# Another table of turns for a fused attention and MLP block on one core

## The chip, the core and the metric

The kernel runs on one core of a Trainium2 chip. Its metric is the device time in microseconds (us) of one execution; lower is better. The engines are named as in the profile: PE is TensorE's matmul (PEld its weight loads), DVE VectorE, ACT ScalarE, POOL GpSimd, SP SyncE, which issues most DMAs.

## The reference

The block normalizes x (2048 tokens, D = 448), computes an attention in four segments of 512 tokens with a memory carried from segment to segment, and a gated MLP beside it, and multiplies the two:

```python
def phi(t): return jnp.where(t > 0, t + 1.0, jnp.exp(t))
for s in range(4):                       # 16 heads of 28
    logits = jnp.einsum('bhqd,bhkd->bhqk', qs, ks) * scale + mask   # causal in the segment
    a_dot = jnp.einsum('bhqk,bhkd->bhqd', _softmax(logits), vs)
    num = jnp.einsum('bhld,bhde->bhle', phi(qs), M)
    den = jnp.einsum('bhld,bhd->bhl', phi(qs), z)[..., None] + 1e-06
    outs.append(g * (num / den) + (1.0 - g) * a_dot)                # g = sigmoid(beta)
    M = M + jnp.einsum('bhld,bhle->bhde', phi(ks), vs); z = z + phi(ks).sum(over l)
s = concat(outs) @ wo
g = silu((gelu(xn @ w_gate) * (xn @ w_up)) @ w_down)                # w_gate: 448 x 1792
return x + s * g
```

## The kernel before

Everything stays in SBUF. A segment has four blocks of 128 tokens; heads are padded from 28 to 32, four to a group of 128 partitions, so there are four groups; the hidden dimension has 14 blocks of 128. PSUM is two pairs of banks (pp) and four single banks (ps). All work is first recorded as 1172 named operations with their dependencies; nothing is emitted then. The function arrange (L158) goes through the table TURNS (L89), one name for each operation, and places every operation at its turn. A suffix such as ":ACT" chooses an engine where two could do it. At its turn an operation also takes its PSUM banks and buffers: of those that its kind may use, the one that by a small cost model comes free first. Then the program emits the operations in that order. The table thereby fixes the order of each engine's own instructions, SP's DMA issues included; every engine works through its instructions in order, and waits at one whose inputs or buffers aren't ready, with all that is behind it on that engine. Engines run freely against each other.

The names that matter here (a number such as 013 is segment 0, hidden block 13; sc07 is segment 0, step 7):

- x1, x2, x3 (L427 for x2 and x3, L353 for x1): the loads of a segment's input, issued by SP. wg8 and wu8 (L353): halves of the gate and up weights. tk and tq (L630), tr (L552): DMA transposes of kT, qT and of the normalized input, also on SP. wo_in (L422), wd_in (L430): the output and down weights.
- bn, ag, ep (L495, L497, L508): statistics, their aggregate and the variance of the layer norm on DVE, pw (L513) the power on POOL, xn (L520) the normalized rows. In segment 0 xc (L530) centres the rows on DVE, and PE transposes these (trc).
- wq, wk, wv (L581): projections in 3 matmuls of 128 rows; wr (L581): the remaining 64 rows. evwq, evwk, evwv (L617): their evacuations. phwq, phwk, miwk (L704 to L709, L696): the two halves of phi.
- sc (L848): scores of one step, four 32-row tiles by two banks; ex (L863): their exponential on ACT; mk (L874): the causal mask on POOL; pv (L910): the product with the values. ou (L746) evacuates the sums.
- gi, gu (L971 in segment 0, L1001 later): gate and up products; ge (L1009): gelu on ACT; hm (L1014): the product of gate and up on DVE, which frees the bank of up. gates: sigmoid of beta on ACT, ahead of the first exponential. dn (L1057, L1123 for the last block): the down product.
- up (L725) updates the memory, rd (L761) reads it; den, dc, rd and rb (L749 to L794) carry the denominators over DRAM; ca, cb (L816, L811 and L819) combine; wo (L1087, L1111) is the output projection, fm, th, sg, fa, y (L1062 to L1142) the tail of a block.
- wo0 (L391): a memset of the output weights' tile; bd0 to bd3 (L417): four small memsets of the mask of the memory. nrm and nrm2: the guard, a check of the weights' norms whose answer the program loads ahead of the last piece of the output (L1184).

## Time and profile before

| what | us |
|---|---|
| median of 3 runs | 225.86 (225.45 to 225.96) |
| the profiled execution | 225.30 |
| its span in the profile | 223.5 |
| DVE busy | 150.9 |
| ACT busy | 158.3 |
| POOL busy | 126.3 |

The profile is one execution. Times in it count from the start of its span; the execution is 1.8 us longer than the span. A row of its timeline has the start, the duration, the engine, the line of the kernel, the operation with output and inputs, the form, how many instructions are joined in the row, and in brackets the idle time of the engine before it and what ended that. Rows of an engine's queue (SPq) are the issues of DMAs, not the transfers.

### The profile page before, as it was taken

Reading aid. Unit: us, or ns where it says so; the run is one execution under the profiler, and the core shown is the slowest. Engines: PE = TensorE matmul, PEld = TensorE weight load, DVE = VectorE, ACT = ScalarE, POOL = GpSimd, SP = SyncE. Lnnn points to the kernel's source line nnn. Section 1 sums busy time; section 2 is a strip of 40 time slices with the busy share of each in tenths; the row PEclk is TensorE's granted clock in tenths of the full one; section 3 lists DMA queues with packets and bytes.
Section 4 is the critical chain, followed back from the end, with each engine's and each line's share of the span. In section 5 each row is a group of like instructions: output and inputs, shape, how many; then the busy total and the mean of one; then the engine's idle time right before and its main releaser. Section 6 shows DMA issues by size and latency. Waiting matters only on the chain.

```text
span 223.5 us, 5109 instructions
## 1 busy us (share of the span) xinstructions
PE 215.4 (96%) x1906; PEld 96.2 (43%) x1906; DVE 150.9 (68%) x285; ACT 158.3 (71%) x218; POOL 126.3 (57%) x219
## 2 busy tenths in 40 slices
PE   7999999899999999999999999999999999999991
PEld 2454343343433354444444444444444434444570
DVE  4586897997779977554688476675835563466472
ACT  5888455899988977959688988744688877436120
POOL 5423100167978889524769995728059767464700
PEclk9999999999999999999999999999999999999999
DMA  6999589896692664326550422083502001448011
GB/s 201 241 345 284 99 126 290 223 164 129 143 130 42 173 177 89 67 67 179 165 133 10 87 64 64 24 221 105 167 21 72 28 14 23 143 120 215 17 45 50
DMA packets 45463, 27.71 MB, mean 124 GB/s; under 512 B 30664, under 2 KB 40840, under 8 KB 45432
## 3 DMA queue, kind: packets, MB, share of 16 engines
q1 hardware_dynamic: 44216, 26.33, 50.9%
q10 hardware_dynamic: 1216, 0.98, 1.3%
q8 instruction: 17, 0.28, 0.5%
q14 instruction: 14, 0.11, 0.2%
HBM read 17.38 MB, written 2.98 MB: 91 GB/s over the span
## 4 chain that ended last, share of the span: by engine, by line
PE 83%; DVE 7%; ACT 4%; issue 2%; DMA 1%; POOL 1%; DVEq 0%; ACTq 0%; POOLq 0%
PE ps L1057 15%; PE ps L1001 14%; PE pp L1001 14%; PE ps L581 12%; PE ps L1087 5%; PE pp L971 5%; PE pp L848 5%; PE ps L971 4%; PE ps L910 4%; ACT pt L863 3%; PE pp L1057 1%; PE ps L761 1%; PE ps L725 1%; DVE st L495 1%; DMA x_sb<-in_A_x_dram 1%
## 5 line engine op out<-in xcount | busy, mean ns | idle before, releaser
L863 ACT ACTIVATE pt<-pp 128x1024 bf16<-128x1024 f32 x76 | 74.0, 1032 | 13.1 <-PE pp L848 12.0
L874 POOL TENSOR_SCALAR_AFFINE_SELECT pt<-pt 128x256 bf16<-128x256 bf16 x128 | 52.7, 443 | 24.0 <-ACT pt L863 23.4
L1057 PE MATMUL ps<-wd_sb,hT 128*128 128x448 bf16 x196 | 41.1, 353 | 0.1
L1014 DVE TENSOR_TENSOR hT<-gl,ps 128x512 bf16<-128x512 bf16 x28 | 18.8, 683 | 19.5 <-ACT gl L1009 19.5
L1009 ACT ACTIVATE gl<-pp 128x512 bf16<-128x512 f32 x28 | 16.6, 597 | 19.6 <-PE pp L1001 14.8
L1001 PEld LDWEIGHTS <-wu_sb 64*128 64x128 bf16 x252 | 23.1, 94 | 14.9
L1001 PEld LDWEIGHTS <-wg_sb 64*128 64x128 bf16 x252 | 23.1, 94 | 14.8 <-issue 1.5
L1057 PEld LDWEIGHTS <-hT 128*128 128x128 bf16 x210 | 19.2, 98 | 20.0 <-issue 3.9
L1009 ACT ACTIVATE gl<-ps 128x512 bf16<-128x512 f32 x28 | 16.5, 596 | 14.0 <-PE ps L1001 9.9
L1014 DVE TENSOR_TENSOR hT<-gl,pp 128x512 bf16<-128x512 bf16 x28 | 18.7, 677 | 7.3 <-ACT gl L1009 7.3
L581 PEld LDWEIGHTS <-xnT 128*128 128x128 bf16 (+1 forms) x192 | 14.4, 96 | 20.3 <-issue 11.4
L772 POOL TENSOR_TENSOR om<-om,rb 128x512 f32<-128x512 f32 x12 | 15.0, 1265 | 13.4 <-DMA rb<-rdr 9.2
L696 POOL TENSOR_SCALAR e<-e 128x896 bf16<-128x896 bf16 (+1 forms) x12 | 11.8, 985 | 15.9 <-ACT e L691 15.9
L819 POOL TENSOR_TENSOR oT<-oa,om 128x512 bf16<-128x512 f32 x12 | 17.3, 1448 | 5.1 <-DVE oa L816 5.1
L513 POOL TENSOR_TENSOR rs<-rs,nhalf 128x1 f32<-128x1 f32 (+1 forms) x7 | 5.3, 763 | 24.7 <-DVE rs L508 24.6
L1001 PE MATMUL ps<-xnT,wg_sb 64*128 64x512 bf16 x66 | 17.8, 377 | 0.0
L1001 PE MATMUL ps<-xnT,wu_sb 64*128 64x512 bf16 x66 | 17.8, 377 | 0.0
L1001 PE MATMUL ps<-xn,wu_sb 64*128 64x512 bf16 x66 | 17.8, 376 | 0.0
L1001 PE MATMUL ps<-xn,wg_sb 64*128 64x512 bf16 x66 | 17.8, 376 | 0.0
L848 PE MATMUL pp<-qT,kT 32*128 32x384 bf16 (+3 forms) x244 | 16.8, 300 | 0.5 <-DVE hT L1014 0.3
L746 DVE COPY oa<-ps 128x512 f32<-128x512 f32 x16 | 10.7, 687 | 9.5 <-PE ps L910 9.0
L1001 PE MATMUL pp<-xnT,wu_sb 64*128 64x512 bf16 x60 | 16.2, 376 | 0.0
(137 smaller groups left out, 449.5 us busy)
## 6 DMA issues: line engine op xcount, KB each, us to landing
rb<-rdr SPq DMA_DIRECT2D x28, 256.0 KB
out_dram<-oo SPq DMA_DIRECT2D x15, 112.0 KB
wd_sb<-in_B_w_down_dram SPq DMA_DIRECT2D x2, 784.0 KB
x_sb<-in_A_x_dram SPq DMA_DIRECT2D x3, 448.0 KB
xn<-xnT SPq DMA_DIRECT2D x6, 192.0 KB
rdr<-dc SPq DMA_DIRECT2D x28, 32.0 KB
wg_sb<-in_B_w_gate_dram SPq DMA_DIRECT2D x2, 384.0 KB
wu_sb<-in_B_w_up_dram SPq DMA_DIRECT2D x2, 384.0 KB
```

Source lines behind the costliest of these rows:

```text
L581: nc.tensor.matmul(out=self.bank.ap()[:, 0:D], lhsT=self.xT.ap()[r, c, n * P:(n + 1) * P], rhs=self.w[r, c, :], **kw)
L696: o = gps(f"mi{nm}{s}{half}", n / 1024, lambda: nc.gpsimd.tensor_scalar(out=t(), in0=t(), scalar1=1.0, scalar2=0.0, op0=ALU.min, op1=ALU.max),
L772: oU[s, g, 1] = t, gps(f"sm{s}{g}", 1.22, lambda t=t, r=r: nc.gpsimd.tensor_tensor(out=t.ap(), in0=t.ap(), in1=r.ap(), op=ALU.mult), deps= ...
L819: oT[s][1].append(gps(f"cb{s}{g}", 1.22, lambda g=g, t=t, tm=tm: nc.gpsimd.tensor_tensor(out=dst.ap()[:, g, :], in0=t.ap(), in1=tm.ap(), o ...
L848: nc.tensor.matmul(out=S2[i // 2].ap(i % 2)[:, c0:c0 + n], lhsT=kT[s][0].ap()[r, g, kb * P:(kb + 1) * P], rhs=qT[s][0].ap()[r, g, kb * P:L ...
L863: nc.scalar.activation(out=dst, in_=src, func=ACT.Exp, scale=scale)
L874: nc.gpsimd.affine_select(out=v, in_=v, pattern=[[0, 2], [1, P]], compare_op=ALU.is_ge, fill=0.0, base=0, channel_multiplier=-1)
L971: m = nc.tensor.matmul(out=bf[fc].ap(i), lhsT=w, rhs=xT.ap()[r, c, :], start=not part and c == 0, stop=bool(part) and c == NC3 - 1)
L1001: nc.tensor.matmul(out=bf[fc].ap(i), lhsT=w, rhs=x, start=c == 0, stop=c == 2 * NC3)
L1009: got[fc] = nc.scalar.activation(out=gl.ap(), in_=bf[fc].ap(0), func=ACT.Gelu_apprx_tanh)
L1014: nc.vector.tensor_tensor(out=hT[s][0].ap()[:, fc, :], in0=gl.ap(), in1=bf[fc].ap(1), op=ALU.mult), deps=[a] + held,
L1057: nc.tensor.matmul(out=bank.ap()[:, 0:D], lhsT=hT[s][0].ap()[:, fc, b * P:(b + 1) * P], rhs=wd_sb[:, fc, :], start=(fc == 0), stop=(fc == ...
```

## The change

Only the table TURNS is another one; it has two lines fewer, so each line number behind it is lower by two in the changed kernel. It holds the same 1172 operations, with other turns and in some cases another engine. No function differs. The first line, and one of the middle:

```diff
 TURNS = """
-red_z nhalf xc_z kn1 ez0 ident qs2 x00 x02 x01 wv wk table su2 su3 warm va0 va1 ones vb1 warm_up bn00 ag00 xc0
...
-gi011 gi012 gu010 ge010 gi013 gu011 gu012 tr13 ge011 x2 wo_in0 wd_in1 tr11 bn22 bn23 bn21 bn20 hm010 hm011
...
+hm08 ge09 hm09 gi011 gi012 wo_in1 bn20 gu010 gi013 ag20 ge010 bn22 bn21 hm010 bn23 ag23 ag21 bd3 gu011 ge011
```

The table comes from a search over disturbed copies of the program, in which PE's inputs are to be ready some time ahead of it. Three places follow as the engines see them.

On SP, from the load of x1 (x_sb_64) to that of x2 (x_sb_65), between 10 and 31 us of the profile; kT_102 and qT_100 are the transposed keys and queries of segment 0, xnT_99 the normalized input of segment 1. Before:

```order
L353 DMA x_sb_64<-in_A_x_dram 128x4x448
L353 DMA wg_sb<-in_B_w_gate_dram 128x3x768
L353 DMA wu_sb<-in_B_w_up_dram 128x3x768
L630 DMA_TRANSPOSE kT_102<-kn_86 128x4x128 x3
L630 DMA_TRANSPOSE qT_100<-hT 128x4x128 x4
L353 DMA betac<-in_A_beta_dram 128x1x1
L630 DMA_TRANSPOSE kT_102<-kn_86 128x4x128
L552 DMA_TRANSPOSE xnT_99<-xn_96 128x4x128 x2
L427 DMA x_sb_65<-in_A_x_dram 128x4x448
L422 DMA wo_sb<-in_A_wo_dram 28x4x448
L430 DMA wd_sb<-in_B_w_down_dram 128x7x448
```

After:

```order
L351 DMA x_sb_64<-in_A_x_dram 128x4x448
L628 DMA_TRANSPOSE kT_102<-kn_86 128x4x128
L351 DMA wg_sb<-in_B_w_gate_dram 128x3x768
L628 DMA_TRANSPOSE kT_102<-kn_86 128x4x128 x2
L351 DMA wu_sb<-in_B_w_up_dram 128x3x768
L628 DMA_TRANSPOSE kT_102<-kn_86 128x4x128
L628 DMA_TRANSPOSE qT_100<-hT 128x4x128 x4
L351 DMA betac<-in_A_beta_dram 128x1x1
L550 DMA_TRANSPOSE xnT_99<-xn_96 128x4x128 x2
L425 DMA x_sb_65<-in_A_x_dram 128x4x448
L425 DMA x_sb_66<-in_A_x_dram 128x4x448
```

The two weight halves went from ahead of the transposes of kT to between them, all four of these stand ahead of qT's, and the load of x3 (x_sb_66) follows x2 directly.

On DVE, the stretch that begins with the statistics of x2 (st, mv: one of each for each block of 128 tokens; hT from gl is hm010 to hm013; kn_86 is the second half of phi for the keys of segment 0, rs the variances). Before, from 34.76 us of the profile on:

```order
L495 BN_STATS st_140<-x_sb_65 128x6
L495 BN_STATS st_137<-x_sb_65 128x6
L495 BN_STATS st_139<-x_sb_65 128x6
L495 BN_STATS st_138<-x_sb_65 128x6
L1014 TENSOR_TENSOR hT<-gl_129,ps_94 128x512
L1014 TENSOR_TENSOR hT<-gl_130,ps_95 128x512
L497 BN_AGGR mv_141<-st_138 128x2
L1014 TENSOR_TENSOR hT<-gl_128,pp_90 128x512
L497 BN_AGGR mv_141<-st_139 128x2
L497 BN_AGGR mv_141<-st_137 128x2
L1014 TENSOR_TENSOR hT<-gl_129,pp_91 128x512
L709 SCALAR_TENSOR_TENSOR kn_86<-kn_86,e_105 128x32x28
```

After, from the second row of that stretch (the first statistic stands right ahead of it) to the one ahead of hm013:

```order
L495 BN_AGGR mv_141<-st_139 128x2
L493 BN_STATS st_140<-x_sb_65 128x6
L493 BN_STATS st_138<-x_sb_65 128x6
L1012 TENSOR_TENSOR hT<-gl_129,ps_95 128x512
L493 BN_STATS st_137<-x_sb_65 128x6
L495 BN_AGGR mv_141<-st_137 128x2
L495 BN_AGGR mv_141<-st_138 128x2
L1012 TENSOR_TENSOR hT<-gl_130,ps_94 128x512
L1012 TENSOR_TENSOR hT<-gl_128,pp_90 128x512
L495 BN_AGGR mv_141<-st_140 128x2
L506 TENSOR_SCALAR rs_143<-mv_141 128x4
L1012 TENSOR_TENSOR hT<-gl_129,pp_91 128x512
```

One hm went ahead of the fourth statistic; the last hm now stands behind all four aggregates and the variances. The second half of phi moved ahead of the stretch.

On POOL, the masks around step 9 of segment 0 (pt is the exponential of one step, e the half-made phi). Before:

```order
L874 AFFINE_SELECT pt3_111<-pt3_111 128x2x128
L874 AFFINE_SELECT pt2_110<-pt2_110 128x2x128
L874 AFFINE_SELECT pt3_111<-pt3_111 128x2x128
L417 MEMSET bdmask_80 28x32
L874 AFFINE_SELECT pt0_108<-pt0_108 128x2x128
L417 MEMSET bdmask_80 28x32
L874 AFFINE_SELECT pt0_108<-pt0_108 128x2x128
L417 MEMSET bdmask_80 28x32
L874 AFFINE_SELECT pt4_112<-pt4_112 128x2x128 x4
L696 TENSOR_SCALAR e1_106<-e1_106 128x1024
```

After:

```order
L694 TENSOR_SCALAR e0_105<-e0_105 128x32x28
L872 AFFINE_SELECT pt2_110<-pt2_110 128x2x128 x3
L872 AFFINE_SELECT pt3_111<-pt3_111 128x2x128 x4
L872 AFFINE_SELECT pt0_108<-pt0_108 128x2x128
L872 AFFINE_SELECT pt2_110<-pt2_110 128x2x128
L872 AFFINE_SELECT pt1_109<-pt1_109 128x2x128
L872 AFFINE_SELECT pt4_112<-pt4_112 128x2x128 x2
L872 AFFINE_SELECT pt0_108<-pt0_108 128x2x128
L872 AFFINE_SELECT pt4_112<-pt4_112 128x2x128 x2
L694 TENSOR_SCALAR e0_105<-e0_105 128x1024
```

The memsets of bdmask (bd1 to bd3) left this place, two for the first 14 us of the program and one for the place of the statistics of x2, and the masks stand in a row between the two halves of phi.

Elsewhere, in words: on POOL the memset wo0 stands at the start, ahead of the first power of the layer norm. On PE the first scores (sc00) are followed by wq11, wv10 and wq10 ahead of sc01, where wk10's and wk11's remainder, wq11 and wv10 stood. The value products pv17 and pv19 go from behind gu12 to behind gu17, pv27 and pv29 from behind gu21 to behind gu26, with the combines of segments 1 and 2 behind them; evwv12 goes ahead of phwq10 on DVE, and pv32 and rd30 earlier on PE. At the end two of the last block's sums (fa330, fa332) are POOL's, its copy es33 DVE's, and the guard's answer is loaded while the last piece is awaited.

125 lines of the change are left out of this document (62 added, 63 removed).

## The prediction

> **What bounds the kernel now.** I read the page of the profile first: the busy times and the chain that ended last.
>
> ```profile
> PE 215.4 (96%) x1906; PEld 96.2 (43%) x1906; DVE 150.9 (68%) x285; ACT 158.3 (71%) x218; POOL 126.3 (57%) x219
> PE 83%; DVE 7%; ACT 4%; issue 2%; DMA 1%; POOL 1%; DVEq 0%; ACTq 0%; POOLq 0%
> ```
>
> TensorE (PE) is busy 215.4 of the span's 223.5 us and is 83% of the chain. The change leaves all 1906 matmuls as they are, so 8.1 us is all that any order could win, and most of that is start and tail. The next view, busy time by stretches, says where PE idles.
>
> ```profile
> 5.30:34.00 28.70, 28.70 (x248) 13.04 (x250) 22.00 (x57) 20.00 (x39) 7.12 (x13) 1.00 0.92 223
> 34.00:45.00 11.00, 10.20 (x77) 3.54 (x71) 10.05 (x24) 8.49 (x13) 1.02 (x1) 1.00 1.02 252
> 45.00:64.00 19.00, 18.58 (x189) 8.12 (x188) 14.75 (x33) 18.81 (x26) 15.73 (x39) 1.00 1.00 148
> 64.00:115.00 51.00, 50.90 (x464) 22.14 (x463) 37.43 (x64) 40.37 (x47) 34.05 (x52) 1.00 0.51 125
> 162.00:184.00 22.00, 21.63 (x185) 9.03 (x185) 12.18 (x21) 18.34 (x22) 16.24 (x29) 1.00 0.12 34
> ```
>
> The columns after the length are PE, PE's weight loads, DVE, ACT and POOL busy, then the granted clock (full), DMA share and GB/s. Between start and tail PE idles 0.80 us at 34 to 45, 0.42 at 45 to 64, 0.10 and 0.37 later: about 1.7 us by this count. It is what a better order can win there. The view of waits names the causes:
>
> ```profile
> PE ps L910 <- POOL pt L874: 0.4, 1, 0.4
> PE ps L848 <- DVE e L617: 0.4, 1, 0.4
> PE pp L848 <- DVE hT L1014: 0.3, 1, 0.3
> ```
>
> So PE waited once for a causal mask on POOL (mk091c0), once for an evacuation and once for a product hm on DVE. The view counts only whole waits; smaller ones show in the distances of matmuls below.
>
> **The change part by part.** All edits move work; none adds or removes arithmetic. I go through the places where PE waits, in order of time.
>
> *The start (0 to 5.3 us).* POOL's memset of wo_sb (op wo0) moves from the middle of segment 0 to the start, ahead of four smaller ones, and lies beside the four products xc0 to xc3 on DVE.
>
> ```profile
> 17.24 1.59 POOL L391 MEMSET wo_sb<- 128x1792 bf16 x1
> 4.11 0.34 DVE L530 TENSOR_SCALAR hT<-x_sb,mv 128x448 bf16<-128x448 bf16 x1
> 6.53 0.57 POOL L513 TENSOR_TENSOR rs<-rs,nhalf 128x1 f32<-128x1 f32 x1 [2.90 <-DVE rs L508]
> ```
>
> POOL sat idle 2.90 us ahead of its first power at 6.53, so 1.59 fits. I take 0 for the place. The bounds: a gain of 0.2, since bn01 now stands behind xc2 and xc3 and the second transposition comes earlier, and a loss of 1.6, if DVE were held through all of the memset (see the rivals).
>
> *The queue of loads (9 to 35 us).* This is SP's row of issues:
>
> ```profile
> 10.09 1.13 SPq L353 DMA_DIRECT2D x_sb<-in_A_x_dram  x1
> 11.27 0.88 SPq L353 DMA_DIRECT2D wg_sb<-in_B_w_gate_dram  x1
> 12.19 1.75 SPq L353 DMA_DIRECT2D wu_sb<-in_B_w_up_dram  x1
> 14.07 6.02 SPq L630 DMA_TRANSPOSE kT<-kn  x3
> 20.19 5.13 SPq L630 DMA_TRANSPOSE qT<-hT  x4
> 26.03 1.27 SPq L630 DMA_TRANSPOSE kT<-kn  x1
> ...
> 29.97 1.11 SPq L427 DMA_DIRECT2D x_sb<-in_A_x_dram  x1
> ```
>
> SP issues without a gap from 10 to 31 us and the DMA engines are 0.92 busy, so x2 (the input of segment 2, issued at 29.97) comes when what is ahead has drained. After the change the very same thirteen transfers stand between x1 and x2; only their order differs: a transposition of kT goes ahead of the two weight halves. Two things can shift x2. The first transposition now waits for its data, up to 2 us in which nothing new is issued (from 11.3 to some 13.3, an estimate from the 14.07 at which it is issued now); if the engines run dry meanwhile, x2 comes later. And the slow issues (2.0 us for one transposition of the three against 1.27 for a lone one) may go, which brings it earlier: three times 0.7 and the 1.75 back to 0.88 would be 3 us, less the 2 us of waiting: 1.0. I take x2 0.3 us earlier, near the unchanged amount of bytes, with −1.0 and +0.9 as ends. The weight halves come up to 5 us later; their first reader is the gate product of hidden block 8 near 27 us, so that is covered.
>
> *The stage behind x2 (34 to 45 us).*
>
> ```profile
> 34.76 2.21 DVE L495 BATCH_NORM_STATS2 st<-x_sb 128x6 f32<-128x448 bf16 x4 [1.24 <-DMA x_sb<-in_A_x_dram]
> 36.89 1.27 DVE L1014 TENSOR_TENSOR hT<-gl,ps 128x512 bf16<-128x512 bf16 x2
> 38.89 0.65 DVE L1014 TENSOR_TENSOR hT<-gl,pp 128x512 bf16<-128x512 bf16 x1
> 39.60 0.39 PE L848 MATMUL pp<-qT,kT 32*128 32x512 bf16 x2 [0.27 <-DVE hT L1014]
> 39.92 0.36 PE L581 MATMUL ps<-wk_sb,xnT 64*128 64x448 bf16 x2
> 40.22 1.04 PE L581 MATMUL ps<-wq_sb,xnT 128*128 128x448 bf16 x5
> ...
> 41.86 0.40 PE L848 MATMUL pp<-qT,kT 32*128 32x384 bf16 x8
> 42.19 1.04 PE L581 MATMUL ps<-wv_sb,xnT 128*128 128x448 bf16 x5
> ```
>
> DVE idles 1.24 us for x2, then does four statistics (2.21, 0.55 each), then the last four products hm of segment 0; the last ends at 39.54 and frees the bank into which the second half of the first scores (sc00, 39.60) goes. After the change hm010 stands behind three statistics and one small aggregate instead of four statistics: some 0.4 earlier. But hm013, the last, has one more aggregate and the small rs ahead of it (ag22 and ep20 came behind it before), and three aggregates now follow straight on a statistic that they read, which ends the overlap of neighbours. I take 0.6 later against x2 as an estimate, near one statistic's 0.55 for five such breaks, between 0.2 (two small instructions alone) and 0.8. With x2 at the same moment sc00's second half moves by +0.6. PE's order behind it changes too: between sc00 and sc01 stand nine matmuls of full height and two of half height, where there were six and four in the 41.86 − 39.60 = 2.26 us. A full one of 448 columns takes some 0.2 (1.04 for five, with the tail of the last); two half ones take 40.22 − 39.92 = 0.30. So 3 × 0.2 − 0.30 and a shape change less: +0.2. Together +0.8, less the 0.3 by which x2 comes earlier: **+0.5** for sc01 and the exponentials behind it, with −0.2 and +1.7 as ends. Part of it is taken by PE's wait for evwq10 (0.4 in the waits above), whose wait would then lie inside the shift: I count **+0.3** on PE.
>
> *The masks (56 to 64 us).*
>
> ```profile
> 56.52 3.95 POOL L874 TENSOR_SCALAR_AFFINE_SELECT pt<-pt 128x256 bf16<-128x256 bf16 x8
> 60.53 0.12 POOL L417 MEMSET bdmask<- 28x32 bf16 x1
> ...
> 62.02 1.48 POOL L874 TENSOR_SCALAR_AFFINE_SELECT pt<-pt 128x256 bf16<-128x256 bf16 x4
> 63.56 0.40 PE L910 MATMUL ps<-pt,vaug 128*32 128x384 bf16 x6 [0.42 <-POOL pt L874]
> 58.91 1.30 DVE L709 SCALAR_TENSOR_TENSOR kn<-kn,e 128x896 bf16<-128x896 bf16 x1
> ```
>
> The value product of step 9 (63.56) waits for the last of four masks, which ends at 63.50, though the backlog is POOL's own: three small memsets between masks (with their gaps some 0.2 each), and eight masks that took 3.95 where four took 1.48, so 1.0 too much, beside the DVE multiply of 58.91. After the change the memsets stand 20 us earlier or more, the multiply comes earlier, and the four masks come some 1.5 us earlier against their exponentials. **−0.42**, and 0 if the exponentials are 0.5 later and all of it is eaten. From here to the tail PE is nearly always bound by its own work, so what is won ahead stays won.
>
> *The later places.*
>
> ```profile
> 67.39 0.40 PE L848 MATMUL pp<-qT,kT 32*128 32x256 bf16 x8
> 67.90 0.35 PE L581 MATMUL ps<-wv_sb,xnT 128*128 128x448 bf16 x1
> 176.10 0.39 PE L761 MATMUL ps<-pqT,mbd 128*128 128x512 bf16 x1
> 176.64 1.67 PE L1087 MATMUL ps<-wo_sb,oT 128*128 128x448 bf16 x8
> ```
>
> Behind the eight scores of 67.39 the projection wv21 starts 0.51 later, where the eight wider ones of 41.86 are followed after 0.33 (42.19): at least 0.18 of waiting for an evacuation that now goes ahead of phi on DVE: **−0.18**. One read of 512 columns is followed after 0.54 by the output projection, whose own start distance is some 0.2 (1.67 for eight): 0.33 of waiting for the bank that ou300 empties; it goes, as the read and the pv ahead of it stand earlier: **−0.33**. Segments 1 and 2 get their pv17, pv19, pv27 and pv29 five hidden blocks later, and with them the whole chain of denominators over DRAM to the output projection. What hides the chain is the rest of that segment's gate and up products and the first down products; PE is fully busy there now. I cost it at nothing; if that cover fails, PE waits for a bank or for oT once, up to some 1 us as an estimate (the longest such waits in the rows above are 0.3 to 0.4).
>
> *The tail.*
>
> ```profile
> 219.10 0.26 DVEq L1184
> ```
>
> The load of the guard's result, 0.26 on DVE's queue, stood between the last-but-one and the last piece of the output; now two of the last sums go to POOL. **−0.1**, between −0.3 (all of the 0.26) and +0.3 (a sum on POOL that takes longer than DVE's).
>
> **The sum:** 0 + 0.3 − 0.42 − 0.18 − 0.33 − 0.1 = −0.73, say −0.8, on the profiled execution's 225.3 (span 223.5 and 1.8 around it): 224.5. That execution lies 0.56 under the median of the runs, 225.86, so on the median it is **225.1**. Differences under 0.2% (0.45 us) cannot be told from no change, so faster begins at 225.41.
>
> **Rivals.** *The loads come later, slower than before.* If SP's 2 us of waiting at 11.3 leaves the DMA engines idle, x2 lands 0.9 later; from +0.4 on, hm013 is late by over 1 us, sc01 by up to 1.7, and at 45 to 64 us ACT (18.81 of 19.00 busy) has no room to catch up. Then PE loses 1.7 less the 0.4 of the wait for evwq10, 1.3 in place of 0.3, and the sum is −0.73 + 1.0 = +0.3, and +0.7 with the masks' gain gone: **226.1 to 226.5**. For it: DMA share 0.92 and no gap on SP. Against: with such a backlog the engines have work for 2 us.
>
> *Nothing gained in the middle.* The exponentials' shift of 0.5 eats what the masks win: −0.73 + 0.42 = −0.3, **225.5**. For it: ACT 18.81 of 19.00.
>
> *A port between DVE and POOL.* If wo0 starts 0.5 ahead of xc0 (4.11 before), as its place behind the other memsets makes likely, and holds DVE until its end, xc0 and the first projection are 1.1 late. PE has no idle time from 5.3 to 34 to take that up, and 0.3 to 1.1 of it stays behind the wait for x2: **225.4 to 226.2**. Against it here: a product of the same form and tile (L520, at 7.14, 0.40) started inside a memset of POOL (7.05 to 7.25).
>
> ```profile
> 7.05 0.20 POOL L391 MEMSET e<- 128x128 bf16 x1
> 7.14 0.40 DVE L520 TENSOR_SCALAR xn<-x_sb,mv,rs 128x448 bf16<-128x448 bf16 x1
> ```
>
> The Trainium skill, page "SBUF — State Buffer", section "SBUF: two separate sides", says that the two engines share one port pair as "an exclusive lock", held for a whole instruction by whichever starts first, with a vector operation of two SBUF inputs in it only against a GpSimd one that reads SBUF. By that rule the eight masks slowed beside the two-input multiply, and the trace agrees with the 3.95; for a memset, which reads nothing, only a fast vector mode could collide, and the row at 7.14 shows no hold.
>
> *The table brings more:* x2 1.0 earlier, so sc01 0.2 earlier, −0.2 in place of +0.3: −1.2, **224.6**.
>
> **Chances:** the forecast 0.40 (224.7 to 225.4), more 0.19, nothing in the middle 0.17, later loads 0.17, the port 0.07. Faster is the first two (0.59), nearly; within 0.2% takes the third and part of the port and of the forecast's upper edge; slower the fourth and part of the port. The range of 8 in 10 reaches from 224.0 (the second case, with the tail's −0.3 in place of −0.1, the start's −0.2, and the 0.25 by which the runs of before lie about their median) to 226.4.
>
> **What would show it.** Right: in the waits of after the row of POOL masks is gone, PE's idle time at 45 to 64 is under 0.2; the first statistics of x2 start at 33.8 to 34.8; sc01 starts between 41.7 and 42.6; the read and the output projection behind it lie 0.22 apart. Wrong: the wait of DVE for x2 grows, PE idles over 1.2 us at 34 to 45, a new row of waits at the output projections of segments 1 or 2, or a first projection after 6 us.

## The result, and the profile after

The changed kernel is slower. Its median is 228.03 us (16 runs, 226.64 to 229.56) against 226.31 us (16 runs, 225.45 to 227.74) for the kernel before, a ratio of 1.0079 (95% interval 1.0058 to 1.0100), or some 1.7 us. The forecast was 225.1, with 224.0 to 226.4.

Two things are to be kept in mind with the traces. Executions of one and the same kernel scatter by over 1 us, as much as a single wait is worth. And the two profiled executions lie on opposite sides: before's at 225.30 is 1.0 under its median, after's at 229.33 (span 227.6) is 1.3 above. Their distance of 4.0 us is more than twice the real one. From the page of after, busy times and the engines' shares of the chain that ended last:

```profile
PE 218.0 (96%) x1906; PEld 98.8 (43%) x1906; DVE 155.1 (68%) x285; ACT 154.4 (68%) x214; POOL 128.7 (57%) x221
PE 73%; DMA 9%; DVE 6%; POOL 5%; issue 2%; ACT 2%; SPq 1%; POOLq 0%; ACTq 0%; DVEq 0%
```

The number of matmuls is the same, but PE is busy 2.6 us longer, and its share of the chain fell from 83 to 73%: DMA and POOL came in. The waits of PE:

```profile
PE ps L461 <- POOL bdmask L415: 0.8, 1, 0.8
PE ps L1055 <- DVE om L744: 0.6, 1, 0.6
PE ps L999 <- ACT gl L1007: 0.3, 1, 0.3
PE ps L999 <- DVE hT L1012: 0.3, 1, 0.3
PE ps L579 <- DMA xnT<-xn: 0.3, 1, 0.3
...
PE ps L908 <- DVE oa L744: 0.3, 1, 0.3
```

The mask on POOL (0.4 before) is gone, as forecast. In its place stand a wait at the start, ahead of the first transposes (0.8, where before had 0.4; its releaser is a case for care, below), and five of 0.3 to 0.6. Windows of after, with the columns of the prediction's window view:

```profile
5.30:37.50 32.20, 32.10 (x266) 14.82 (x268) 24.87 (x65) 20.42 (x39) 6.06 (x13) 1.00 0.95 217
37.50:47.00 9.50, 8.95 (x66) 3.27 (x61) 9.35 (x23) 8.09 (x13) 1.43 (x2) 1.00 0.89 231
47.00:66.00 19.00, 19.00 (x192) 8.41 (x188) 15.75 (x35) 18.83 (x26) 16.29 (x35) 1.00 1.09 147
66.00:91.00 25.00, 23.70 (x209) 10.15 (x209) 19.84 (x33) 19.21 (x22) 18.30 (x28) 1.00 0.53 117
91.00:119.00 28.00, 27.30 (x257) 12.49 (x252) 15.71 (x26) 18.64 (x25) 14.55 (x22) 1.00 0.43 102
```

PE idles 0 at 47 to 66, where it idled 0.42 before: that gain is there. But it idles 1.30 at 66 to 91 and 0.70 at 91 to 119, where before had 0.10 in all of 64 to 115. New gaps opened behind the place that was mended.

A sharper ruler than the windows are the score blocks on PE, of which each segment has ten, always in the same sequence. Where a block of after starts, less where that of before starts, is how late PE is there. Start rows of four blocks in the timeline, before:

```profile
61.60 0.39 PE L848 MATMUL pp<-qT,kT 32*128 32x512 bf16 x4
...
86.71 0.40 PE L848 MATMUL pp<-qT,kT 32*128 32x384 bf16 x8
...
109.60 0.39 PE L848 MATMUL pp<-qT,kT 32*128 32x512 bf16 x4
...
182.83 0.34 PE L848 MATMUL pp<-qT,kT 32*128 32x384 bf16 x2
```

and after:

```profile
63.40 0.39 PE L846 MATMUL pp<-qT,kT 32*128 32x512 bf16 x4
...
89.25 0.40 PE L846 MATMUL pp<-qT,kT 32*128 32x384 bf16 x8
...
113.38 0.40 PE L846 MATMUL pp<-qT,kT 32*128 32x512 bf16 x4
...
186.77 0.34 PE L846 MATMUL pp<-qT,kT 32*128 32x384 bf16 x2
```

These are sc10, sc19, sc20 and sc39. After is 1.80 late at sc10, 2.54 at sc19, 3.78 at sc20, 3.94 at sc39: it loses at the start, between sc10 and sc19 (the scores of segment 1, +0.74), and between sc19 and sc20 (the gate and up products, +1.24). Behind sc20 next to nothing is lost. The experiments follow these three places; the kernels' lateness at the four blocks is in a table behind them.

### The profile page after: what moved, and what is told of

Its sections match the earlier page's. It is cut to its first block, busy times and chain, and to the rows that moved or that the text cites. A ratio compares the mean times of both kernels' runs of the same rounds, so it can differ in the third digit from the quotient of the medians.

```text
span 227.6 us, 5105 instructions
## 1 busy us (share of the span) xinstructions
PE 218.0 (96%) x1906; PEld 98.8 (43%) x1906; DVE 155.1 (68%) x285; ACT 154.4 (68%) x214; POOL 128.7 (57%) x221
## 4 chain that ended last, share of the span: by engine, by line
PE 73%; DMA 9%; DVE 6%; POOL 5%; issue 2%; ACT 2%; SPq 1%; POOLq 0%; ACTq 0%; DVEq 0%
PE ps L1055 17%; PE ps L999 14%; PE pp L999 11%; PE ps L579 9%; PE pp L846 5%; PE ps L908 4%; PE ps L1085 4%; PE pp L969 3%; PE ps L969 2%; DMA rb<-rdr 2%; DMA x_sb<-in_A_x_dram 2%; DMA qT<-e 2%; POOL oT L809 2%; DVE hT L1012 2%; PE pp L579 1%
## 5 line engine op out<-in xcount | busy, mean ns | idle before, releaser
L872 POOL TENSOR_SCALAR_AFFINE_SELECT pt<-pt 128x256 bf16<-128x256 bf16 x128 | 54.2, 456 | 16.3 <-ACT pt L861 16.1
L1055 PE MATMUL ps<-wd_sb,hT 128*128 128x448 bf16 x210 | 44.3, 353 | 0.8 <-DVE om L744 0.6
L1012 DVE TENSOR_TENSOR hT<-gl,ps 128x512 bf16<-128x512 bf16 x29 | 19.6, 681 | 19.6 <-ACT gl L1007 18.7
L999 PEld LDWEIGHTS <-wu_sb 64*128 64x128 bf16 x252 | 23.0, 94 | 14.8 <-issue 0.6
L999 PEld LDWEIGHTS <-wg_sb 64*128 64x128 bf16 x252 | 22.5, 94 | 15.6 <-issue 2.9
L770 POOL TENSOR_TENSOR om<-om,rb 128x512 f32<-128x512 f32 x12 | 16.6, 1403 | 19.7 <-DMA rb<-rdr 18.9
L1012 DVE TENSOR_TENSOR hT<-gl,pp 128x512 bf16<-128x512 bf16 x27 | 18.0, 679 | 5.6 <-ACT gl L1007 5.6
L1076 POOL TENSOR_TENSOR oo<-sg,x_sb 128x448 bf16<-128x448 f32 (+2 forms) x14 | 13.4, 967 | 14.3 <-issue 6.2
L999 PE MATMUL ps<-xnT,wg_sb 64*128 64x512 bf16 x69 | 18.8, 377 | 0.3 <-ACT gl L1007 0.3
L999 PE MATMUL ps<-xnT,wu_sb 64*128 64x512 bf16 x69 | 18.6, 377 | 0.3 <-DVE hT L1012 0.3
L999 PE MATMUL ps<-xn,wu_sb 64*128 64x512 bf16 x69 | 18.6, 376 | 0.0
L999 PE MATMUL ps<-xn,wg_sb 64*128 64x512 bf16 x69 | 18.6, 376 | 0.0
L846 PE MATMUL pp<-qT,kT 32*128 32x384 bf16 (+3 forms) x244 | 16.9, 300 | 0.6 <-DVE hT L1012 0.3
L817 POOL TENSOR_TENSOR oT<-oa,om 128x512 bf16<-128x512 f32 x12 | 15.2, 1266 | 3.6 <-DVE oa L814 3.6
```

What stands on the lines that cost most here:

```text
L770: oU[s, g, 1] = t, gps(f"sm{s}{g}", 1.22, lambda t=t, r=r: nc.gpsimd.tensor_tensor(out=t.ap(), in0=t.ap(), in1=r.ap(), op=ALU.mult), deps= ...
L817: oT[s][1].append(gps(f"cb{s}{g}", 1.22, lambda g=g, t=t, tm=tm: nc.gpsimd.tensor_tensor(out=dst.ap()[:, g, :], in0=t.ap(), in1=tm.ap(), o ...
L846: nc.tensor.matmul(out=S2[i // 2].ap(i % 2)[:, c0:c0 + n], lhsT=kT[s][0].ap()[r, g, kb * P:(kb + 1) * P], rhs=qT[s][0].ap()[r, g, kb * P:L ...
L872: nc.gpsimd.affine_select(out=v, in_=v, pattern=[[0, 2], [1, P]], compare_op=ALU.is_ge, fill=0.0, base=0, channel_multiplier=-1)
L999: nc.tensor.matmul(out=bf[fc].ap(i), lhsT=w, rhs=x, start=c == 0, stop=c == 2 * NC3)
L1012: nc.vector.tensor_tensor(out=hT[s][0].ap()[:, fc, :], in0=gl.ap(), in1=bf[fc].ap(1), op=ALU.mult), deps=[a] + held,
```

## Experiments: the start

The rival of the shared port was told by one edit in each direction: take only the memset wo0 back in the changed kernel, and bring only wo0 forward in the kernel before.

**wo0 back to its later place, in the changed kernel.**

```diff
-trc00 xc3 evc00:ACT wo0 vb0 bn01 trc02
+trc00 xc3 evc00:ACT vb0 bn01 trc02
...
-gi06 miwk01 miwk00 sq5 pw10
+gi06 miwk01 miwk00 wo0 sq5 pw10
```

> The changed table, with one turn altered: the memset wo0 goes back to the middle of segment 0, behind miwk00. Theory S (the start): wo0 held xc0 (1.23 us instead of 0.34), PE idled 0.75 us and then worked at half its rate until 9.1 us; that put PE 2.0 us back at 34 us, and 1.6 of it stayed. Then this kernel is 1.6 to 2.0 us faster than the changed one: 226.0 to 226.4, ratio to the kernel before about 1.00, xc0 lasts 0.34, the first projection starts at 5.8. Rival A (absorbed): x2 bounds the stage anyway, so the start is worth under 0.4 us: 227.6 or more.

The timeline of after at the start:

```profile
3.29 1.59 POOL L389 MEMSET wo_sb<- 128x1792 bf16 x1
4.11 1.23 DVE L528 TENSOR_SCALAR hT<-x_sb,mv 128x448 bf16<-128x448 bf16 x1
4.82 0.37 POOL L409 MEMSET vaug<- 128x64 bf16 x1
...
5.39 1.46 PE L461 MATMUL ps<-oT,hT 128*128 128x128 bf16 x12 [0.75 <-POOL bdmask L415]
...
6.68 1.30 PE L579 MATMUL ps<-wv_sb,xnT 128*128 128x448 bf16 x3
7.78 1.33 PE L579 MATMUL pp<-wv_sb,xnT 128*128 128x448 bf16 x3
```

and of the experiment:

```profile
3.92 0.34 DVE L528 TENSOR_SCALAR hT<-x_sb,mv 128x448 bf16<-128x448 bf16 x1
...
4.45 1.48 PE L461 MATMUL ps<-oT,hT 128*128 128x128 bf16 x12
```

With the memset beside it, the product xc0 takes 1.23 in place of 0.34, to 0.46 after the memset's end (3.29 + 1.59 = 4.88). PE then starts its transposes at 5.39 and not at 4.45. The bracket names POOL's bdmask, but the transposes read hT, which xc0 writes: the releaser is inferred, and the last to end by name was a bystander. The time: 227.67 (12 runs), 1.0050 to before (1.0017 to 1.0083). By this pair 0.29 of the 0.79% lies here, but a single pair is uncertain by some 0.4; later crosses measure the same edit again.

**wo0 forward in the kernel before.**

```diff
-wr0 sv3 kn0 vb0 ep00 pw00
+wr0 sv3 kn0 wo0 vb0 ep00 pw00
...
-ge04 miwk00 bd wo0 pw10
+ge04 miwk00 bd pw10
```

> The kernel before, with one turn altered: the memset wo0 goes to the start, ahead of vb0. Theory S: xc0 lasts 1.2 us, the first projection comes 0.9 later and at half rate; the kernel is 1.2 to 2.0 us slower than before (ratio 1.005 to 1.009), though its queue of loads has the old order. Rival A (absorbed, or the loads' new order was needed for the loss): within 0.4 us of before.

226.45 (12 runs), 1.0013 (0.9986 to 1.0039): no change that can be told. The memset came at 3.25 and took 1.60. xc0, which started at 4.24, took 0.74: it was held for 0.40 only and ended 0.13 behind the memset. Its later start does not explain that: it began 0.99 into the memset, and in h1 below a product that began 0.92 into it was held for 0.80. Why it was held less here stays open. PE's first transposes followed at 5.04 (4.51 in before), and at sc10 its trace is 0.41 late, which the interval neither shows nor excludes.

**A longer warm-up.** After also ran its first projections at half the rate (1.30 for three of 448 columns, 0.73 before). If the gap of 0.75 ahead of the transposes causes that, more warm-up matmuls in it should cure it.

```diff
-            for i in range(8):
+            for i in range(13):
```

> The changed table, wo0 still early, with 13 warm-up matmuls instead of 8, which fill PE's idle time from 4.4 to 5.4 us (their results are overwritten). If the half rate came from the idle time, the transpositions at 5.4 and the projections behind run at full rate (448 columns in 0.19 us) and the first wk starts at 10.1 instead of 11.2: 1.0 to 1.2 us faster than the changed kernel, about 226.9. If all of the loss is the hold of xc0, or the half rate has another cause, it stays within 0.3 of the changed kernel's 228.0.

227.83 (12 runs), 1.0061 (1.0032 to 1.0089): nothing won. The 13 warm-up matmuls ran without a gap and at half rate until 6.6 us; only what came behind them was at full rate. The gap is therefore not what keeps the rate down.

**The memset in four parts.** If the two engines take turns by instruction, four memsets of 448 columns should let xc0 in after the first.

```diff
-        wo_z = fill("POOL", "wo0", 1.55, -70, wo_sb[:], 0.0)
+        wo_z = op("wo0", {"POOL": (1.55, 1.61)}, lambda: [nc.gpsimd.memset(wo_sb[:, i, :], 0.0) for i in range(4)], prio=-70)
```

> The changed table with the memset wo0 as four memsets of 448 columns, 0.4 us each, at the same place. If POOL holds DVE for the length of one instruction, xc0 waits for one of them at most: its duration falls from 1.23 to 0.4 to 0.8 us, PE's first transposition comes at 4.5 to 4.9 instead of 5.4, and the kernel is 0.3 to 0.9 us faster than the changed one (227.1 to 227.7). If the hold lasts as long as POOL has memsets to do, xc0 stays at 1.2 and the time at 228.

```profile
3.29 1.71 POOL L418 MEMSET wo_sb<- 128x448 bf16 x4
4.08 1.38 DVE L528 TENSOR_SCALAR hT<-x_sb,mv 128x448 bf16<-128x448 bf16 x1
4.94 0.38 POOL L409 MEMSET vaug<- 128x64 bf16 x1
```

xc0 took 1.38, again to 0.46 after the end of the last memset, as with one memset: it is not let in between instructions that follow each other at once. 228.91 (6 runs), 1.0115 (1.0072 to 1.0158).

## Experiments: which half of the table costs

pv09 is the value product behind the masks, whose wait was forecast to go. The two tables can be cut behind it and crossed.

**The changed order up to pv09, the rest in before's order.**

As an edit of the changed kernel, at the seam; what follows is before's order of whatever is not yet done:

```diff
-ex101 tr30 tr33 pv09 ou020 den020 wk20 wv12 ou030 den030
+ex101 tr30 tr33 pv09 gates2 tr32 ou020 ou030 mk100c0 wv12
...
```

> A table made of both: the changed one up to pv09 (65 us of its profile), and from there what is left in the order of the kernel before. Theory L (the loss lies in the later places, 68 to 97 us: wq32 waiting for a transpose 0.5, dn030 for ou101 0.66, pv14 for ou100 0.39, the output projection 0.25, the gelu behind exwk21 1.0; 2.6 to 2.8 us in three profiles): none of these is in it, the mask's wait of 0.6 is gone, and the start and x2 cost 0.5 to 1.5 at 54 us. Then it is within 0.5 us of the kernel before (ratio 0.998 to 1.003). Theory S2 (the loss lies in the start and the loads up to 65 us): it is as slow as the changed kernel, 1.006 to 1.010.

227.86 (12 runs), 1.0075 (1.0046 to 1.0104).

**Before's order up to pv09, the rest in the changed order.**

As an edit of the kernel before, at the seam; what follows is the changed order of whatever is not yet done:

```diff
-sg02 pv07 pv09 ex100 ex101 ou020 ou030 mk100c0 wv12 nrm2
+sg02 pv07 pv09 wo_in3 nrm2 ex100 ex101 tr33 ou020 den020 wk20 wv12 ou030 den030
...
```

> The other way round: the kernel before up to pv09, then what is left in the order of the changed table. Theory L: it has all the later waits, 2.6 us, less the 0.3 of the read at 176 us: 227.8 to 228.8, ratio 1.007 to 1.011, as slow as the changed kernel or slower. Theory S2: within 0.5 us of before or faster by the 0.3.

227.91 (12 runs), 1.0075 (1.0044 to 1.0105). Each half alone costs about what the whole change costs, so the parts do not add up: either the first half holds a gain beside its loss, or the seams, where two orders meet that were not made for each other, cost something of their own. The next two kernels took the first half apart.

**The first cross, with wo0 late.** The edit is that of the first experiment.

> The first of these four with the memset wo0 back in the middle of segment 0. If the start's hold reaches the end, it is 0.4 to 1.0 us faster than that one and faster than the kernel before by 0.3 to 0.8 (225.5 to 226.0). If x2 bounds the stage behind it, both are equal within 0.3 us.

226.62 (12 runs), 1.0012 (0.9988 to 1.0037): taking wo0 back is worth 1.0075 less 1.0012 here. Yet its trace has a wait that neither parent has. Where two halves meet, two DMA transposes (tr33, tr32) stood ahead of the DMAs of two denominators (den020, den030) on SP. Rows of SP and DVE and of the memory read behind them on PE:

```profile
64.07 3.90 SPq L550 DMA_TRANSPOSE xnT<-xn  x3
68.07 1.11 SPq L747 DMA_DIRECT2D den<-oa  x2
...
72.40 0.36 DVE L781 TENSOR_SCALAR dc<-dc,igate 128x64 f32<-128x64 f32 x1 [2.21 <-DMA dc<-den]
73.88 0.38 PE L759 MATMUL ps<-pqT,mbd 128*128 128x512 bf16 x1 [1.44 <-DVE vaug L615]
```

Three transposes take SP 3.90 to issue, the denominators go out at 68.07, DVE waits 2.21 for them with all that is queued behind (the evacuation vaug among it), and PE waits 1.44 for that.

**The same with the denominators ahead of these transposes.**

```diff
-ex101 tr30 tr33 pv09 gates2 tr32 ou020 ou030 mk100c0
+ex101 tr30 pv09 gates2 ou020 ou030 den020 den030 tr33 tr32 mk100c0
...
-wr2wk0 wv20 den020 ex110 ex111 mk101c0 mk110c384 den030 sc12
+wr2wk0 wv20 ex110 ex111 mk101c0 mk110c384 sc12
```

> The mix of the changed table up to pv09 and the order before from there, wo0 late (0.12% slower than before), with one edit on SP at the seam: the DMAs of the denominators den020 and den030 go ahead of the transposes tr33 and tr32 (2.5 us of issuing). In the mix they were issued at 68.1 instead of 63.7, dg00 waited for them on DVE until 72.4 (before: 69.5), and PE lost 1.9 us behind it at 72 to 74. Theory D (the DVE queue stands behind dg00, which waits for denominators that SP issues late): dg00 comes by 70.7, 1.2 to 1.9 us are won, 224.8 to 225.4, ratio 0.994 to 0.997, faster than the kernel before: the first part of the changed table, without wo0, is a gain. Rival: the landing of den020 isn't set by its place on SP (the denominators' path over DRAM is busy), and the wait stays: 226.4 to 226.8.

```profile
64.24 1.09 SPq L747 DMA_DIRECT2D den<-oa  x2
65.39 2.51 SPq L550 DMA_TRANSPOSE xnT<-xn  x2
...
70.06 0.25 DVE L781 TENSOR_SCALAR dc<-dc,igate 128x64 f32<-128x64 f32 x1 [0.44 <-DMA dc<-den]
71.71 0.38 PE L759 MATMUL ps<-pqT,mbd 128*128 128x512 bf16 x1
```

The denominators go out 3.8 us earlier, DVE waits 0.44, PE not at all. **225.12** (12 runs, 224.71 to 226.58) against 225.94 for before on the same chip: 0.9959 (0.9939 to 0.9979). This kernel beats both. It is the first part of the changed table, without the early wo0 and with before's order from there on. So some 0.9 us can be had with the first part and this seam. How much of it belongs to the seam was not tried: its order of denominators and transposes stands in neither of the two tables (in before, tr32 stands ahead of these two denominators and tr33 behind them), and with the other seam the same first part gained nothing (h1b, 1.0012).

## Experiments: the rest of the table

**The gains of the prediction alone.** Into the kernel before went only three edits, two of them from behind pv09: the small memsets of bdmask early, evwv12 ahead of phi, pv32 earlier.

```diff
-ge04 miwk00 bd wo0 pw10
+ge04 miwk00 bd bd0 bd1 bd2 bd3 wo0 pw10
...
-nrm2 wr1wv2 evwv13 phwq10 sc11 wk20
+nrm2 wr1wv2 evwv13 evwv12 phwq10 sc11 wk20
...
-mk340c384 mk341c384 dn2110 xw30 dn2210
+mk340c384 mk341c384 dn2110 pv32 xw30 dn2210
```

(Each name leaves its old place.) The second of them is an order that the changed table does not have: there phi (phwq10) still goes ahead of evwv12 on DVE, at 65.71, and the evacuations follow at 66.84.

> The kernel before with only the three edits on which the prediction's gains rest: bd0 to bd3 behind bd (out of the masks of step 9), evwv12 ahead of phwq10 on DVE, pv32 ahead of dn2210 (so that ou300 empties its bank earlier). By the prediction's terms: PE's waits at 62.8 (0.42 to 0.59), 67.5 (0.18) and 176 (0.33) go or shrink, 0.7 to 1.0 us in all: 225.2 to 225.6, ratio 0.9955 to 0.997; PE's start of sc39 comes 0.7 to 1.0 earlier against gu013. Rival: the gains are absorbed by what comes next (ACT's row of exponentials, DMA): within 0.3 us of before.

226.09 (12 runs), 1.0000 (0.9975 to 1.0025). The waits they aimed at shrank or moved (PE's wait for the mask is gone from the view; a projection now waits 0.3 for the sums that ou empties), and the time did not move by more than 0.25% either way. **The last two of these edits on top of the fastest mix:**

> The same with evwv12 ahead of phwq10 and pv32 ahead of dn2210, the two later gains of the prediction (0.18 and 0.33). If they stay, 0.3 to 0.5 us under the one before it; if what follows absorbs them, the same within 0.3.

225.48 (12 runs), 0.9988 (0.9967 to 1.0008), where the mix without them gave 0.9959: no gain from evwv12 and pv32.

**Two waits of the changed order taken away.** In after, dn030 on PE waited 0.6 for a bank that ou101 empties, and ou101 stood on DVE behind the product dc and its reciprocal, which wait for a DMA of denominators. It stood behind them in before too, but there the product (at 69.50) did not wait. Two moves made the wait: on SP the last two denominators go out behind two transposes, at 67.10, where before sent them at 63.11; and on PE the read rd10, whose bank ou101 empties, now goes ahead of dn030, which takes that bank next. Timeline of after:

```profile
71.49 0.74 DVE L781 TENSOR_SCALAR dc<-dc,igate 128x64 f32<-128x64 f32 x1 [0.93 <-DMA dc<-den]
72.27 0.55 DVE L785 RECIPROCAL dc<-dc 128x64 f32<-128x64 f32 x1
72.74 0.63 DVE L744 COPY om<-ps 128x512 f32<-128x512 f32 x1
...
73.42 1.11 PE L1055 MATMUL ps<-wd_sb,hT 128*128 128x448 bf16 x5 [0.58 <-DVE om L744]
```

Here ou101 goes ahead of the waiting product, and the projection wq32, which waited 0.3 for a transpose, behind wr2wv2.

```diff
-mk100c0 sc12 wv23 wq32 evwv21
+mk100c0 sc12 wv23 evwv21
...
-ex120 dg00 rc00 mk111c0 ex121 rd001 rd002 ou101
+ex120 mk111c0 ex121 ou101 dg00 rc00 rd001 rd002
...
-rd000 wv22 wr2wv2 sc13
+rd000 wv22 wr2wv2 wq32 sc13
```

> The changed table with two of the later waits taken away: wq32 behind wr2wv2 (it waited 0.5 us for the transpose of xnT's block 2 of segment 3), and dg00, rc00 and two of the reads' DMAs behind ou101 (ou101 waited on DVE behind dg00, which waited for the denominators from DRAM; dn030 on PE waited 0.66 for its bank). Theory L: 0.8 to 1.1 us faster than the changed kernel, about 227.0, and the two waits are gone from the list. Rival: the wait of dg00 only moves on to the combine of segment 0 (cb00, ou100, pv14, then 0.5 longer), so under 0.4 us are won.

228.47 (11 runs), 1.0094 (1.0060 to 1.0128). Both waits are gone from its trace, and a new one of 1.1 stands at the value product pv12 a little later (`PE ps L908 <- DVE kn L615`), so from sc10 to sc19 it loses 0.23 in place of 0.74; the median shows no gain at all. The new wait is of the edit's own making: an operation takes its bank at its turn, and with wq32 elsewhere some sixty operations behind it get another one. pv12 now takes the bank of wk23, which evwk23 on DVE has to empty first; in after it had one of its own. All five kernels with this edit of wq32 (f1, and x2, y1, y2, z1 below) wait there for 0.99 to 1.07. So none of the five shows what taking the two waits away is worth by itself, and ou101 ahead of the product with wq32 in its place was not run.

**The exponential of phi ahead of the first gelu.** Between sc19 and sc20 the first gelu comes late. ACT in before:

```profile
89.16 1.28 ACT L1009 ACT_TABLE_LOAD   x1
90.45 0.60 ACT L1009 ACTIVATE gl<-ps 128x512 bf16<-128x512 f32 x1
...
92.40 1.28 ACT L691 ACT_TABLE_LOAD   x1
93.69 0.95 ACT L691 ACTIVATE e<-kn 128x896 bf16<-128x896 bf16 x1
94.66 1.28 ACT L1009 ACT_TABLE_LOAD   x1
```

and in after:

```profile
93.24 0.95 ACT L689 ACTIVATE e<-kn 128x896 bf16<-128x896 bf16 x1 [1.61 <-DMA qT<-e]
94.21 1.28 ACT L1007 ACT_TABLE_LOAD   x1
95.50 0.60 ACT L1007 ACTIVATE gl<-ps 128x512 bf16<-128x512 f32 x1
```

Before broke the run of gelus for exwk21 (the exponential of phi for keys of segment 2), which costs two more loads of ACT's table. The changed table puts exwk21 ahead of all gelus. That saves the two loads, but exwk21 has to wait 1.61 for a buffer that a DMA transpose (tq22) still reads, and the first gelu starts 6.25 behind sc19 where it started 3.74 behind it. Meanwhile the gate and up products fill their banks, and PE waits twice (the two rows of 0.3 at L999 above). In this kernel tq22 and its evacuation go earlier:

```diff
-ou100 ex161 um1 tk23 wr2wq0
+ou100 ex161 um1 wr2wq0
...
-sc18 evwq21 evwq23 den131 den100 wo02
+sc18 evwq21 evwq23 evwq22 den131 wo02
...
-fa02 ex180 ex181 evwq22 tq21 sc19
+fa02 ex180 ex181 tq21 sc19
...
-fm01 ex190 tq22 dc11
+fm01 ex190 tq22 den100 tk23 dc11
```

> The changed table with one wait attacked: exwk21 stands ahead of ge10 on ACT and waits for the transpose tq22 to have read its buffer. Here evwq22 goes behind evwq23 on DVE, out of its place behind fm02, and on SP tk23 and den100 go behind tq22, so that tq22 is issued some 2 us earlier. Theory L: exwk21 no longer waits, ge10 comes 1.2 to 1.6 earlier and the two waits of PE for a gelu at 95 to 97 us (1.0 together) go: 1.0 faster than the changed kernel, about 227.0. Rival: den100 behind tq22 makes the combine of segment 1 late, and the wait comes back at its output projection: within 0.3 us of the changed kernel.

```profile
92.20 0.95 ACT L689 ACTIVATE e<-kn 128x896 bf16<-128x896 bf16 x1
93.17 1.28 ACT L1007 ACT_TABLE_LOAD   x1
...
94.46 0.60 ACT L1007 ACTIVATE gl<-ps 128x512 bf16<-128x512 f32 x1
```

exwk21 no longer waits, and sc20 is just as late as sc19 (3.23 and 3.23): in this execution the loss of 1.24 is gone. (Other kernels with the same edit still lost 0.50 to 0.73 there, in the table below.) The time is 228.20 (8 runs), 1.0082 (1.0047 to 1.0117), no better than after.

**exwk21 behind ge11, with wo0 late**, that is, with before's two more table loads:

```diff
-mk171c0 exwk21 gu12 miwk21 mk190c384
+mk171c0 gu12 mk190c384
...
-hm10 ge12 ge11 hm11
+hm10 ge12 ge11 exwk21 miwk21 hm11
```

> The changed table, with wo0 late as in the first run, and exwk21 and miwk21 behind ge11, as in the kernel before (in the changed one exwk21 stands ahead of ge10 on ACT, waits there 1.6 us for a transpose of qT, and PE waits twice 0.5 us at 95 to 97 us for a gelu). Theory L: those 1.0 us are lost besides the start: 225.0 to 225.4, 1.0 under the first run. Rival: the wait only moves, since exwk21 and two more table loads then stand ahead of ge13: within 0.3 of the first run.

228.61 (6 runs), 1.0096 (1.0058 to 1.0135). The waits at 96 are gone; waits of up to 1.2 appeared at the scores of segment 2 (`PE pp L846 <- DVE hT L1012: 1.7, 2, 1.2`). In this execution the loss only moved.

**Several of these at once.** First x1's edit with wo0 late and wq32 behind wr2wv2:

> The second of these with wo0 late (0.4 to 1.2 us in the runs so far) and wq32 behind wr2wv2 (its wait for a transpose was 0.5 to 0.8). If start, wq32 and exwk21 are the loss, all is undone: 225.5 to 226.3, no slower than before (ratio 0.997 to 1.001). If it stays over 1.004, a good part of the loss is in none of them.

227.28 (12 runs), 1.0042 (1.0017 to 1.0066). Then ou101 as well (the edits of f1 and x1, wo0 late):

> The changed table with everything undone that the traces blame: wo0 late; wq32 behind wr2wv2 and dg00, rc00 behind ou101; evwq22 early and tk23, den100 behind tq22. If start, dg00 on DVE and exwk21 on ACT are all of the loss, it is back at the kernel before or under it by the gains of the middle: 225.6 to 226.6, ratio 0.997 to 1.001, and PE's position against the kernel before grows by under 0.5 us from 58 to 183 us. If it stays over 1.003, a further part of the table costs time.

227.13 (12 runs), 1.0036 (1.0007 to 1.0064); its trace keeps one wait of 1.06 at pv12. The same with wo0 early:

> The same with wo0 at the start as in the changed table. The difference to the one before is the start alone: by the hold of xc0 (0.5 to 0.9) and a half rate that lasts longer in some executions, 0.6 to 1.2 us slower than that one. If the start is absorbed by x2's landing, under 0.3.

227.68 (12 runs), 1.0074 (1.0043 to 1.0105). The second cross (before up to pv09) with the edits of f1 and x1:

> The kernel before up to pv09 and the changed order from there, with the three waits undone as in the first of these. The mix without these edits was 0.75% slower than before. If dg00, wq32 and exwk21 are the loss of the later part, this one is within 0.4 us of before (ratio 0.998 to 1.002). If it stays at 1.005 or more, the loss of the later part lies elsewhere, and is the same in all executions.

228.82 (6 runs), 1.0113 (1.0079 to 1.0148), worse than the cross without them. Last, the changed order with wo0 late, x1's edit and tr33 behind den030, the move that had helped the mix:

> The changed table with wo0 late, evwq22 early with tk23 and den100 behind tq22, and tr33 behind den030 on SP. Theory D: dg00 comes 1.2 us earlier against PE, the waits of wq32's neighbour dn030 (0.3 to 0.7) and of pv14 (0.3 to 0.4) shrink, and PE's position grows by under 0.3 us from 58 to 87 us where it grew by 0.7 to 0.8; 226.2 to 226.8, ratio 1.000 to 1.003. If it stays at 1.004 or more, the loss between 65 and 90 us isn't that of the denominators.

227.34 (6 runs), 1.0072 (1.0045 to 1.0098): no help here. The denominators go out at 63.63 in place of 66.28 (e1), but the two transposes then stand ahead of the load that brings them back (67.46), and the product dc still waits 0.84.

How late PE was in the profiled execution of each kernel but e4 and x2, against that of before (start of the score block, less 61.60, 86.71, 109.60 and 182.83):

| kernel | at sc10 | sc10 to sc19 | sc19 to sc20 | sc20 to sc39 | ratio to before |
|---|---|---|---|---|---|
| after | 1.80 | +0.74 | +1.24 | +0.16 | 1.0079 |
| wo0 late (e1) | 0.66 | +0.71 | +1.19 | +0.63 | 1.0050 |
| longer warm-up (e5) | 1.08 | +0.77 | +0.94 | +0.15 | 1.0061 |
| wo0 in four (y4) | 0.60 | +0.68 | +1.30 | +0.58 | 1.0115 |
| before, wo0 early (e2) | 0.41 | +0.02 | 0.00 | 0.00 | 1.0013 |
| three small edits (g3) | 0.79 | −0.53 | 0.00 | +0.18 | 1.0000 |
| two waits undone (f1) | 0.42 | +0.23 | +1.30 | +0.67 | 1.0094 |
| earlier tq22 (x1) | 2.45 | +0.78 | 0.00 | +0.16 | 1.0082 |
| y1 | −0.34 | +0.23 | +0.73 | +0.15 | 1.0036 |
| y2 | 0.16 | +0.91 | +0.50 | +0.16 | 1.0074 |
| w3 | −0.14 | +0.81 | +0.55 | +0.16 | 1.0072 |
| before, then changed (h2) | 1.14 | −0.25 | +0.98 | +0.15 | 1.0075 |
| h2 with the edits of f1 and x1 (z1) | 0.99 | +1.96 | +0.60 | +0.16 | 1.0113 |
| changed, then before (h1) | 0.87 | +1.40 | 0.00 | −0.01 | 1.0075 |
| h1 with wo0 late (h1b) | 1.11 | +1.40 | 0.00 | 0.00 | 1.0012 |
| the fastest mix (w1) | 0.55 | −0.48 | +0.01 | −0.01 | 0.9959 |
| w1 with two gains (w2) | −0.46 | −0.32 | 0.00 | +0.18 | 0.9988 |

The table is read by columns. From sc19 on, before's order keeps its distances to 0.01 us from one execution to the next; the changed order loses 0.94 to 1.30 there up to sc20 each time, and 0.00 to 0.73 where tq22 is moved. Between sc10 and sc19 it loses some 0.6 to 0.8 each time when wq32 is left in its place, but not in h2, behind before's first half; with wq32 moved it loses anything from 0.23 to 1.96. The first column is what scatters: kernels with the same start differ in it by over 1 us. What scatters there is the arrival of the load of x2, as the second point below works out.

## Why the prediction was wrong, point by point

Three differences of the ratios carry the result. *wo0* costs 0.29, 0.38 and 0.63% (after against e1, y2 against y1, h1 against h1b), on average 0.43%, some 1.0 us; single pairs are uncertain by about 0.4. In before's order, where it held xc0 less, it costs 0.13% (e2). *The first part without it* gains 0.41% with the seam of w1, 0.9 us, and nothing with that of h1b. *The rest* costs 0.75% (h2, its own seam included), 1.7 us. Together 1.0 − 0.9 + 1.7 = 1.8, and 1.7 was measured. As each term is uncertain by half a us or more, and the sum would be 2.9 with h1b's seam, it is partly luck that the two meet so closely.

- **The start, "I take 0 for the place": this step failed, by some 1.0 us.** The bound of 1.6 was right, the rival of the port was right in its mechanism (xc0 is held to the end of the memset), and its 225.4 to 226.2 had the right size for this term; its chance of 0.07 was far too low. The reason to discard it was the row at 7.14, a product that started inside a memset. But that memset (7.05, 0.20) ended at 7.25. A hold could have lasted 0.11 us there, which cannot be seen in a product of 0.40. The row was silent, and was read as a witness. "A first projection after 6 us" was named as a sign of being wrong, and it came, at 6.68 (5.76 in before). It tells less than it seems: with wo0 late the changed order has it mostly near 6.25, as it then waits for the load of wv (0.32 in e1). So a good part of the hold is covered there, and by which way wo0 costs 1.0 us stays open.
- **The load of x2 and the stage behind it, +0.3: the sum against x2 was right, the allowance for evwq10 was not, and x2 itself scatters by more than the term.** The first statistics of x2 started at 35.86, not at 33.8 to 34.8, and sc01 at 43.67, not at 41.7 to 42.6:

```profile
15.39 1.31 SPq L628 DMA_TRANSPOSE kT<-kn  x1
...
35.86 0.63 DVE L493 BATCH_NORM_STATS2 st<-x_sb 128x6 f32<-128x448 bf16 x1 [0.83 <-DMA x_sb<-in_A_x_dram]
...
43.67 0.40 PE L846 MATMUL pp<-qT,kT 32*128 32x384 bf16 x8
```

From the first statistics to sc01 it is 7.81 here, and 7.10 in before (34.76 to 41.86). All five kernels with before's order at this stage have 7.09 or 7.10; of the fifteen with the changed order fourteen have 7.81 or 7.82, and e5 has 7.91. So the new order costs 0.71 against x2, where +0.8 was forecast. (The second half of phi, said to have moved ahead of this stretch, stands behind it: it starts at 48.56, at 39.47 in before.) From sc01 to sc10 all kernels but e5 take 19.71 to 19.75, in either order. The wait for evwq10 is gone from the view, but nothing of the 0.71 was taken up by it: sc10's lateness is the arrival of x2 plus that 0.71 (1.10 + 0.71 in after, where 1.80 was measured). The arrival scatters: the first statistics start at 33.60 to 36.51 over all kernels, on average at 35.4 with before's order, 35.1 in the seven with the changed order and wo0 early, and 34.4 with wo0 late (without kernel x2). So the averages bear out the forecast's 0.3 earlier, with too much scatter to show it, while in the execution of after x2 came 1.1 later. SP stood until 15.39 at the first transposition of kT there, where 13.3 was forecast (13.73 in e1). Whether that is what delays x2, as the rival of the later loads has it, is not shown; as DVE came to x2 later too, its wait shrank from 1.24 to 0.83 and tells nothing of the load.
- **The masks, −0.42: right in the trace.** The row of POOL masks is gone, and PE idles 0 there. With the small edit alone in before's order (g3), the stretch from sc10 to the next score block is 0.46 shorter. The median of g3 did not follow, but with ± 0.25% it can hide a gain of this size. So the mask's share of the 0.9 us is read from the trace and not shown by a run.
- **wv21, −0.18, and the read, −0.33: the first came in the trace, the second failed.** In g3 the stretch from sc12 to sc13 is 0.16 shorter, as forecast. The read and its output projection lie 0.23 apart in after (0.22 was forecast), but from sc20 to sc39 after is 0.16 later and not earlier. g3 and w2, in all else before's order there, show why: they lose 0.18 between sc35 and sc39, and the eight matmuls of the output projection behind the read take 1.93 where they took 1.67. The wait moved from ahead of the projection into it. evwv12 and pv32 together gained nothing in the median of w2.
- **The later places, "I cost it at nothing": this step failed, and it is the largest term, +1.7.** The prediction looked at what the moved combines and value products hide behind, and bounded a failing cover by "up to some 1 us" once. It did not go through the three engines that serve PE there. Between sc10 and sc19 (+0.74) the denominators come later from SP's queue, DVE waits for them with ou101 behind, and on PE the read whose bank ou101 empties has come to stand ahead of dn030, which needs that bank. Between sc19 and sc20 (+1.24) exwk21 has come to stand ahead of the first gelu on ACT, where it waits for a buffer. These moves stand in the change; the prediction named none of them.
- **The tail, −0.1: too small to tell.** From sc39 to the end of the span it is 40.8 in after (227.6 − 186.77) and 40.7 in before (223.5 − 182.83).

What is shown and what is not: that wo0 costs time, that the first part gains with w1's seam, and that the rest loses behind before's first half, is shown by crossed kernels and their intervals. That the rest loses by the two waits at dn030 and at the first gelu is argued from traces alone. Taking the second away (x1) brought 1.24 us in its own trace and nothing in the median, and an interval of ± 0.35% can hide about 0.8 us. The first was never taken away cleanly, since f1 and all kernels built on it have the new wait at pv12. In h2 the stage from sc10 to sc19 is not late at all, and its trace accounts for 0.9 us (−0.25 + 0.98 + 0.15) of the 1.7 by which its median is slower. Why the stage is late behind the changed first half, and where the rest of the 1.7 us lies, stays open. y1, which has wo0 late and both waits undone, is still 0.36% (0.8 us) slower than before, about as much as the wait of 1.06 at pv12; that this wait is the cause was not shown.
